# Fetching the weights of the second layer earlier, and v of the first batch one z transpose sooner, in a fused attention and mixer kernel

## Chip, cores, metric

One core of one Trainium2 chip. The metric is the device time of one execution in microseconds (us). Medians and ranges are over several executions. "PE" is the matmul engine, "DVE" VectorE, "ACT" ScalarE, "POOL" GpSimd, "SP" SyncE. Two kinds of DMA matter: copies issued by POOL (queue q0) and transposes issued by SP (queue q1). A DMA "lands" when its last data has arrived. "Half clock" is a stretch in which the clock records of the trace grant PE half its speed. L260 in a profile is line 260 of the kernel.

## The reference

```python
def attn(u, v, z):                    # u, v: (8, 3136, 256), z: (8, 3136, 64)
    scores = z @ z.T / S              # per batch
    return u * (np.maximum(scores, 0) ** 2 @ v)

def moe(x, U, V, w_ch1, w_ch2):       # U: (3136, 32), V: (32, 3136), w: (256, 1024), (1024, 256)
    u = x + (x.T @ U @ V).T
    return u + np.maximum(u @ w_ch1, 0) @ w_ch2
# out = moe(attn(u, v, z), ...)
```

The second layer of a batch needs U, V, w1 and w2. Here it runs beside the attention of the next batch, so the weights are first needed when batch 1 begins, about 125 us into the program.

## The kernel before

A batch is 25 tiles of 128 rows ("steps" i = 0 to 24). The scores are symmetric, so only half the blocks are computed (`A`); the other half (`strip`) is made by DMA transposes, one per step, four steps ahead of use. z of the next batch is transposed by two DMA transposes (`z_half`, `z_turn`). In the second layer, `ut` is made of `x_bf` by further DMA transposes. All transposes are issued by SP in program order; all copies from memory by POOL in program order.

```python
def turn(b, o):                                   # SP: 1536 packets of 256 bytes
    strip = strip_pool.tile([P, HALF, P], BF16)   # 5 buffers
    transpose(out=strip, in_=A[o][:, P:])

def start_up():                                   # the first 8 outputs of batch 0, all at once
    load_z(0, parts); load_v(0, v_parts[0])
    double_z(0, parts)
    turn_z(0, parts)                              # three z transposes
    mark = small.tile(...)
    nc.gpsimd.tensor_copy(out=mark[:1, :1], in_=zT[:1, NF - 1, :1])   # POOL waits for the last of them
    for part in v_parts[1:]:
        load_v(0, part)
    # ... u of the first outputs, z of batch 1, scores and the first four outputs ...
    # ... the next four outputs ...

weights = weight_steps()    # w1, U, V piece, V piece, put, put, w2, V tail, put, put, put, copies
start_up()
weights = dict(zip((8, 9, 13, 14, 15, 16, 17, 18, 19, 20, 21, 22), weights))   # one per step of batch 0
# ...
        z_load, z_double, z_half, z_turn = (1, 5, 7, 11) if b else (None, 9, 11, 13)
        v_at = (1, 3, 4, 5, 7, 8, 10, 11, 12) if b else (8, 9, 10, 14, 15, 16, 17, 18, 19)   # v of the next batch
# scores from the new z begin in step 15 of batch 0:
next_first = ahead_of((15, 15, 15, 16, 16, 17, 18, 19, 20, 21, 22, 23), (15, 16, 17, 18, 19, 20, 21))
```

## Time and profile before

Median 1078.82 us over the first three runs (1078.75 to 1081.77). From batch 2 on a batch takes 126.8 us and PE hardly waits; what there is to gain lies before 145 us.

| wait of PE, kernel before | at (us) | length (us) |
|---|---|---|
| first z transpose | 10.12 | 10.12 |
| v of batch 0 | 17.68 | 1.88 |
| two strip transposes | 69.33, 74.60 | 1.66 + 2.29 |
| second z transpose of batch 1 | 89.36 | 10.21 |
| first ut transpose (second layer of batch 0) | 139.03 | 3.90 |

The timeline of PE of the kernel before, cut to the matmuls that waited for a DMA: start, length, what, and in brackets the idle time before it and what ended that.

```profile
10.12 1.03 PE L260 MATMUL ps<-zT 64*128 64x512 bf16 x4 [10.12 <-DMA zT<-z_bf]
...
17.68 0.50 PE L333 MATMUL ps<-v,v 64*128 64x256 bf16 x6 [1.88 <-DMA v<-in_v_dram]
...
69.33 0.28 PE L333 MATMUL ps<-v,strip 64*128 64x256 bf16 x2 [1.66 <-DMA strip<-A]
...
74.60 1.48 PE L333 MATMUL ps<-v,strip 64*128 64x256 bf16 x24 [2.29 <-DMA strip<-A]
...
89.36 0.24 PE L260 MATMUL ps<-zT 64*128 64x64 bf16 x2 [10.21 <-DMA zT<-z_bf]
...
139.03 0.59 PE L455 MATMUL ps<-ut,w_bf 128*128 128x512 bf16 x1 [3.90 <-DMA ut<-x_bf]
```

The chain of waits of the kernel before between 55 and 92 us, its end: it leaves PE at 61.57 and runs through a strip transpose, 4.2 us of PE and the z transpose.

```profile
61.57 12.98 DMA strip<-A
74.56 0.04 issue
74.60 4.23 PE ps L333 x74
78.83 0.64 SPq L295
79.47 0.05 issue
79.52 9.79 DMA zT<-z_bf
```

The timeline of SP of the kernel before, same stretch: the second number is how long the issues kept SP, with the waits between them where a line has several (in the first line SP waits 5.2 us, until 56.16, for a semaphore). An issue takes 1.4 us when the DMA is free (1.42 us at 26.17, with a DMA share of 0.03 from 26 to 27 us); here the z transpose alone keeps SP for 7.80 us.

```profile
49.36 22.38 SPq L295 DMA_TRANSPOSE strip<-A  x4
71.79 3.39 SPq L184 DMA_TRANSPOSE zT<-z_bf  x1
75.28 4.18 SPq L295 DMA_TRANSPOSE strip<-A  x2
79.52 7.80 SPq L184 DMA_TRANSPOSE zT<-z_bf  x1
```

What the DMA engines did from 80 to 84 us (queue: packets, MB, share of 16 engines' time): copies had 94%, and all transposes together, the one that PE waits for among them, moved 0.02 MB. Times of packets overlap in the trace, so that shares can add up to more than 100%.

```profile
q0 software_dynamic: 292, 0.52, 94.1%
q1 hardware_dynamic: 121, 0.02, 20.4%
```

Three stretches of 40 us of the kernel before. After the length come the busy times (and counts) of PE, weight loads, DVE, ACT and POOL, then the granted PE clock, the DMA share and GB/s. DMA is used least in the first of them, and PE least in the second.

```profile
10.00:50.00 40.00, 33.16 (x458) 25.99 (x460) 27.53 (x54) 33.38 (x53) 7.44 (x15) 1.00 0.77 147
50.00:90.00 40.00, 24.64 (x416) 19.93 (x414) 18.75 (x38) 18.28 (x28) 8.85 (x16) 0.91 1.18 174
90.00:130.00 40.00, 39.62 (x686) 33.05 (x682) 29.97 (x53) 27.08 (x38) 10.42 (x17) 0.96 1.22 189
```

### The profile page before, as it was taken

The page shows a single profiled execution, that of the slowest core. Times are in us where ns is not written, and L with a number is a line of the kernel's source. Part 1 is how long each engine was busy: PE and PEld are TensorE (multiplying, and loading weights), DVE is VectorE, ACT ScalarE, POOL GpSimd, SP SyncE. Part 2 cuts the span into 40 slices and gives each one's busy share as a digit, 9 for nine tenths or more (in the row PEclk, how much of TensorE's full clock was granted, in tenths as well). Part 3 has the DMA queues.
Part 4 walks back from the last instruction along what each step waited for, and adds up shares of the span by engine and source line. Part 5 has one row for each costly group of instructions (what it writes and reads, how often), then busy time and mean ns, then how long its engine had stood idle before and what let it go on. Part 6 is the DMA issues. An engine that isn't in the chain of part 4 may idle for free.

```text
span 1078.5 us, 31056 instructions
## 1 busy us (share of the span) xinstructions
PE 1010.8 (94%) x13789; PEld 792.3 (73%) x13829; DVE 525.7 (49%) x937; ACT 611.7 (57%) x814; POOL 179.0 (17%) x332
## 2 busy tenths in 40 slices
PE   5876989999999999999999999999999999999896
PEld 3665857788677877778777886778777887778564
DVE  4755734456443554446454465435554465432331
ACT  5955655466664666556654666556655566542253
POOL 3022201211121111211212111211112110111011
PEclk9998989999999999999999999999999999999898
DMA  8799999969989798979989789997989887588231
GB/s 142 145 170 190 172 163 169 172 140 169 162 173 176 150 183 163 164 159 167 177 167 173 147 167 160 175 179 150 179 158 171 168 160 134 129 150 168 57 98 64
DMA packets 417174, 168.71 MB, mean 156 GB/s; under 512 B 392768, under 2 KB 402640, under 8 KB 417040
## 3 DMA queue, kind: packets, MB, share of 16 engines
q1 hardware_dynamic: 386464, 96.77, 56.7%
q0 software_dynamic: 30576, 69.96, 27.7%
q8 instruction: 108, 1.77, 0.7%
q14 instruction: 26, 0.21, 0.1%
HBM read 61.88 MB, written 25.69 MB: 81 GB/s over the span
## 4 chain that ended last, share of the span: by engine, by line
PE 77%; DVE 7%; DMA 6%; ACT 5%; issue 3%; POOL 1%; SPq 0%; POOLq 0%; ACTq 0%; DVEq 0%
PE ps L333 40%; PE ps L486 15%; PE ps L455 15%; PE ps L260 5%; ACT A L273 3%; DVE x_bf L435 2%; DMA strip<-A 2%; DVE both L348 2%; DVE A L275 2%; DMA ut<-x_bf 1%; DMA zT<-z_bf 1%; PE ps L401 1%; DVE x_bf L351 1%; ACT both L347 1%; PE ps L421 1%
## 5 line engine op out<-in xcount | busy, mean ns | idle before, releaser
L273 ACT ACTIVATE A<-ps 128x832 bf16<-128x832 f32 (+8 forms) x469 | 351.6, 763 | 184.8 <-PE ps L260 175.5
L333 PE MATMUL ps<-v,A 64*128 64x256 bf16 x5064 | 357.9, 270 | 5.7 <-DVE x_bf L435 2.3
L275 DVE TENSOR_TENSOR A<-A 128x832 bf16<-128x832 bf16 (+8 forms) x469 | 240.5, 524 | 219.1 <-ACT A L273 216.2
L333 PE MATMUL ps<-v,strip 64*128 64x256 bf16 x4612 | 319.3, 269 | 3.9 <-DMA strip<-A 3.9
L462 ACT ACTIVATE relu<-ps 128x1024 bf16<-128x1024 f32 (+2 forms) x224 | 203.5, 917 | 190.5 <-PE ps L455 190.5
L333 PEld LDWEIGHTS <-A 64*128 64x128 bf16 x5064 | 251.5, 94 | 64.0 <-issue 27.3
L333 PEld LDWEIGHTS <-strip 64*128 64x128 bf16 x4612 | 233.3, 94 | 37.8 <-DMA strip<-A 4.5
L455 PE MATMUL ps<-ut,w_bf 128*128 128x512 bf16 (+2 forms) x856 | 205.1, 357 | 11.6 <-DMA ut<-x_bf 6.7
L486 PE MATMUL ps<-w_bf,relu 128*128 128x256 bf16 x1600 | 205.9, 273 | 1.0
L486 PEld LDWEIGHTS <-relu 128*128 128x128 bf16 x1600 | 153.8, 98 | 49.5 <-issue 9.3
L260 PE MATMUL ps<-zT 64*128 64x416 bf16 (+9 forms) x933 | 155.7, 317 | 23.3 <-DMA zT<-z_bf 20.3
L497 DVE TENSOR_TENSOR o_sb<-ps,x_bf 128x512 f32<-128x512 f32 (+1 forms) x104 | 69.7, 670 | 221.2 <-PE ps L486 221.2
L455 PEld LDWEIGHTS <-w_bf 128*128 128x128 bf16 x896 | 87.2, 99 | 69.6 <-issue 18.0
L317 POOL DMA_DIRECT2D u_sb<-in_u_dram x96 | 53.5, 558 | 494.3 <-DVE x_bf L351 440.7
L504 POOL DMA_DIRECT2D out_dram<-o_sb x96 | 52.4, 546 | 330.9 <-DVE o_sb L497 330.9
L347 ACT COPY both<-ps 128x512 f32<-128x512 f32 (+1 forms) x104 | 58.8, 566 | 64.7 <-PE ps L333 64.6
L348 DVE TENSOR_TENSOR both<-ps,both 128x512 f32<-128x512 f32 (+1 forms) x104 | 69.3, 666 | 53.0 <-ACT both L347 52.5
L260 PEld LDWEIGHTS <-zT 64*128 64x128 bf16 x933 | 53.1, 95 | 32.1 <-DMA zT<-z_bf 20.6
L351 DVE TENSOR_TENSOR x_bf<-both,u_sb 128x512 bf16<-128x512 f32 (+1 forms) x104 | 69.8, 671 | 6.3 <-DMA u_sb<-in_u_dram 2.7
L435 DVE TENSOR_TENSOR x_bf<-ps,x_bf 128x512 bf16<-128x512 f32 (+1 forms) x112 | 65.4, 625 | 15.4 <-PE ps L421 15.3
L195 POOL DMA_DIRECT2D v<-in_v_dram x61 | 34.1, 566 | 0.0
L421 PE MATMUL ps<-t_sb,V_bf 64*128 64x256 bf16 x200 | 22.6, 273 | 9.9 <-DVE both L348 8.3
(33 smaller groups left out, 134.2 us busy)
## 6 DMA issues: line engine op xcount, KB each, us to landing
u_sb<-in_u_dram POOLq DMA_DIRECT2D x96, 256.0 KB, 3.5
out_dram<-o_sb POOLq DMA_DIRECT2D x96, 256.0 KB, 3.0
v<-in_v_dram POOLq DMA_DIRECT2D x57, 192.0 KB, 5.9
strip<-A SPq DMA_TRANSPOSE x196, 4.9
z_c<-in_z_dram POOLq DMA_DIRECT2D x7, 384.0 KB, 5.5
w_bf<-in_moe_w_ch_dram POOLq DMA_DIRECT2D x2, 512.0 KB, 7.8
u_sb<-in_u_dram POOLq DMA_DIRECT2D x16, 64.0 KB, 2.2
ut<-x_bf SPq DMA_TRANSPOSE x56, 3.5
```

The source lines that it names most:

```text
L260: mm(out=ps[:, k, :n], lhsT=zT[halves[k], j, :], rhs=zT_flat[halves[k], c : c + n], start=True, stop=True,)
L273: nc.scalar.activation(out=dst, in_=src, func=AF.Relu, scale=sc)
L275: nc.vector.tensor_tensor(out=dst, in0=dst, in1=dst, op=ALU.mult)
L333: mm(out=acc[t0][h][:, (o - t0) * D : (o - t0 + 1) * D], lhsT=w[halves[h]], rhs=v_both[b % 2][halves[h], j, :], start=start, stop=stop, **kw,)
L347: nc.scalar.copy(out=both[:, :w], in_=banks[1][:, :w])
L348: nc.vector.tensor_tensor(out=both[:, :w], in0=banks[0][:, :w], in1=both[:, :w], op=ALU.add)
L351: nc.vector.tensor_tensor(out=x_at(b, t0, n), in0=split(both[:, :w]), in1=u_sb[:, :n, :].rearrange("p t (a c) -> p t a c", c=P), op=ALU.mult,)
L435: nc.vector.tensor_tensor(out=q, in0=split(ps[h][:, : len(ks) * D]), in1=q, op=ALU.add)
L455: mm(out=ps[:, i, :w], lhsT=w1_bf[:, db, (hp + i) * P : (hp + i + 1) * P], rhs=uT[c][:, db, len(chunks[c]) * P - w :], start=(db == 0), st ...
L462: nc.scalar.activation(out=relus[c][:, hp : hp + 2, :w], in_=ps[:, :, :w], func=AF.Relu)
L486: mm(out=ps[:, k * D : (k + 1) * D], lhsT=relus[c][:, ht, q : q + P], rhs=w2_bf[:, ht, :], start=(ht == 0), stop=(ht == NH - 1),)
L497: nc.vector.tensor_tensor(out=o_sb[:p, :nk, :].rearrange("p t (a c) -> p t a c", c=P), in0=split(ps[:p, : nk * D]), in1=x_at(b, t, nk)[:p] ...
```

## The change

Copies that nobody needs before 115 us are moved out of the crowded stretch into the one where DMA had gaps: w1, U and the two large pieces of V go behind z of batch 1 (about 20 us), w2 behind the first four outputs (about 33 us). The marker that holds v of batch 0 back waits for the second z transpose in place of the third. One piece of v of batch 1 moves from step 14 to 12, and the later ones one step sooner.

```diff
+            lambda: wide(w2_bf, moe_w_ch2),          # order of weight_steps: w2 fifth
             lambda: put(0, 0, FIRST),
             lambda: put(0, FIRST, NF),
-            lambda: wide(w2_bf, moe_w_ch2),
...
-        nc.gpsimd.tensor_copy(out=mark[:1, :1], in_=zT[:1, NF - 1, :1])
+        nc.gpsimd.tensor_copy(out=mark[:1, :1], in_=zT[:1, 7, :1])
...
             load_z(1, WHOLE)
+        for s in weights[:4]:
+            s()
...
             load_u(0, o)                             # u of outputs 5 to 8
+        weights[4]()
...
-    weights = dict(zip((8, 9, 13, 14, 15, 16, 17, 18, 19, 20, 21, 22), weights))
+    weights = dict(zip((14, 15, 16, 17, 18, 19, 20), weights[5:]))
...
-        v_at = (...) if b else (8, 9, 10, 14, 15, 16, 17, 18, 19)
+        v_at = (...) if b else (8, 9, 10, 12, 14, 15, 16, 17, 18)
```

More of the change, by code (lines that the diff above doesn't have):

```diff
@@ L683 @@
         soon = next_at if b else next_first
-        v_at = (1, 3, 4, 5, 7, 8, 10, 11, 12) if b else (8, 9, 10, 14, 15, 16, 17, 18, 19)
+        v_at = (1, 3, 4, 5, 7, 8, 10, 11, 12) if b else (8, 9, 10, 12, 14, 15, 16, 17, 18)
         v_at = dict(zip(v_at, V_PARTS))
```

## The prediction

> **What bounds the kernel now.** The page shows PE busy 1010.8 of 1078.5 us. From batch 2 on, PE hardly waits: the same matmul recurs at 264.42, 391.26, 518.31 us (126.8 us a batch). In the PE timeline, waits ended by DMA: 10.12 us (first z transpose), 1.88 us at 17.68 (v of batch 0), 1.66 us at 69.33 and 2.29 us at 74.60 (strip transposes), 10.21 us at 89.36 (second half of the z transpose of batch 1), 3.90 us at 139.03 (first ut transpose). Two are followed by half clock (clock records: 82.9-93.2 and 137.5-144.4 us), costing about 1.9 and 2.7 us more. Batch 1 (131.54 to 264.42) takes 132.9 us against 126.8 later: 6.0 us.
>
> **Why.** Transposes from SP share the DMA engines with copies from POOL. Uncontended, a strip transpose lands in 3.7 us; between 56 and 88 us it takes 8.8 to 13.1, while w1 (7.3 us to landing), U (10.2), two V pieces (6.7, 7.9) and v pieces of batch 1 (8 to 10) are under way. SP issues in order, and an issue that takes 1.4 us free takes 5.3, 6.6 and 7.8 us there; the z transpose that PE needs at 78.7 is issued at 79.52 and lands at 89.31. [...] copies of 1.5 to 6 KB packets leave the 256-byte transpose packets almost nothing at 80-84 us. w2 (8.4 us at 101 us) does the same to strips (9 to 13 us), a backlog reaching to the ut transpose at 131.5.
>
> **What the change moves.** No arithmetic. w1, U and V go to about 20-35 us, w2 to about 34-44 us. There strips are needed only from 42.4 us on. v of batch 0 is released by the second z transpose (10.97) instead of the third (12.35). One v piece of batch 1 moves from the 9th to step 12, later ones one step earlier; V's copies on DVE come a little sooner (1.1 us each).
>
> **Sum on the critical path.** v sooner: -1.4. The two strip waits: -3.9. z wait of 10.2: the earliest issue is about 69.5 us in the new time, behind two strips, and I let about 2 us of wait stay: -8.3. Its half clock: -1.9, less 0.3 left. ACT/strip wait at 117.8: -0.4. Batch 1 to the steady pace: -6.0, less 0.5. New contention at 25-45 us: allow +1. Total about -20.8.
>
> Predicted **1058.0 us**, range 1054.5 to 1064.0. Faster by over 2%: 0.47; within 2%: 0.52; slower: 0.01.
>
> **Seen in the profile if right.** PE's wait for v at 17.7 falls to about 0.5 us. w1, U, V land by 36 us, w2 by 46. Strips at 55-75 us land in 4 to 7 us; SP's issue of the second z transpose comes near 69-70; PE's wait for it is 0 to 4 us. No half clock near 83-93 and 137-144. PE's ut wait gone; batch 1 takes about 127 us.
>
> **What would make it wrong.** Strips of the first outputs (needed from 42 us) or the u pairs held up by w1/w2: a new wait at 42-53 us. The three v pieces and five strips at 54-70 us alone keep the DMA full: z wait stays at 5 us or more and the clock drops. [...]

## The result

Changed kernel: median **1066.20 us** (1065.36 to 1066.61, 4 runs) against 1079.48 us (1078.75 to 1081.77, 4 runs), ratio 0.9872 (95% interval 0.9855 to 0.9890). A ratio here is the mean time of one kernel's fast runs over that of the other's of the same rounds, so it is not quite the ratio of the medians. Executions over 1.5% slower than the fastest of the same kernel are left out of the means. The gain is 13.3 us by the medians; predicted were 20.8. 1066.2 lies outside the predicted range of 1054.5 to 1064.0.

The waits for v, for strips and for ut are gone; of the z wait 6.24 us are left. PE's timeline of the changed kernel, the two matmuls that waited for a DMA before 145 us:

```profile
9.55 1.04 PE L260 MATMUL ps<-zT 64*128 64x512 bf16 x4 [9.55 <-DMA zT<-z_bf]
...
79.44 0.23 PE L260 MATMUL ps<-zT 64*128 64x64 bf16 x2 [6.24 <-DMA zT<-z_bf]
```

The chain of waits of the changed kernel, where it leaves PE; a single transpose is left in it.

```profile
67.09 3.08 PE ps L333 x54
70.17 1.18 SPq L295
71.35 0.05 issue
71.41 0.03 issue
71.44 7.95 DMA zT<-z_bf
```

SP of the changed kernel: the six transposes ahead of the second z transpose are issued in 17 us (54.51 to 71.44) in place of 23 (56.16 to 79.52), but the z transpose itself keeps SP for 5.87 us.

```profile
54.51 9.82 SPq L295 DMA_TRANSPOSE strip<-A  x3
64.38 1.91 SPq L184 DMA_TRANSPOSE zT<-z_bf  x1
66.39 4.96 SPq L295 DMA_TRANSPOSE strip<-A  x2
71.44 5.87 SPq L184 DMA_TRANSPOSE zT<-z_bf  x1
```

POOL of the changed kernel. Look at 69.05 and 69.57: a u load and two v pieces go out 1.3 to 2.4 us ahead of the z transpose at 71.44.

```profile
62.57 0.60 POOL L195 DMA_DIRECT2D v<-in_v_dram  x1
67.17 0.55 POOL L317 DMA_DIRECT2D u_sb<-in_u_dram  x1 [4.00 <-DVE A L275]
69.05 0.54 POOL L317 DMA_DIRECT2D u_sb<-in_u_dram  x1 [1.32 <-DVE x_bf L351]
69.57 1.09 POOL L195 DMA_DIRECT2D v<-in_v_dram  x2
81.59 0.85 POOL L317 DMA_DIRECT2D u_sb<-in_u_dram  x1 [10.93 <-DVE x_bf L351]
```

The same three stretches of the changed kernel: the first now uses the DMA as fully as the next (1.15 for 0.77) and PE did no less in it; PE's busy time in the second rose from 24.6 to 32.6 us.

```profile
10.00:50.00 40.00, 35.15 (x480) 27.59 (x478) 29.15 (x58) 35.02 (x55) 12.04 (x23) 1.00 1.15 192
50.00:90.00 40.00, 32.58 (x533) 26.45 (x529) 24.54 (x46) 23.32 (x37) 7.91 (x14) 0.91 1.17 190
90.00:130.00 40.00, 39.00 (x648) 30.79 (x646) 28.19 (x50) 27.79 (x38) 8.11 (x14) 1.00 1.01 175
```

Where the time of the two profiled runs (1078.5 and 1063.6 us) differs, by four points that both traces have:

| from | to | before | changed | difference |
|---|---|---|---|---|
| start | first matmul on a strip | 42.40 | 40.75 | -1.65 |
| there | end of the z wait | 46.96 | 38.69 | -8.27 |
| there | first matmul of the second layer (x U) | 36.75 | 36.56 | -0.19 |
| there | the same in batch 2 | 132.88 | 127.25 | -5.63 |
| there | end | 819.5 | 820.4 | +0.8 |

The last line is one wait of 1.66 us for a ut transpose at 761 us, partly made up at the end; waits like it stand near 760 us in the profiles of two of the runs below (e14 2.16 us, e18 1.71 us) and not in the others, so it is taken as chance.

### The profile page after: what moved, and what is told of

Read it like the earlier page. It is cut to its first block, busy times and chain, and to the rows that moved or that the text cites. A ratio compares the mean times of both kernels' runs of the same rounds, so it can differ in the third digit from the quotient of the medians.

```text
span 1063.6 us, 31097 instructions
## 1 busy us (share of the span) xinstructions
PE 1010.7 (95%) x13829; PEld 791.3 (74%) x13829; DVE 525.3 (49%) x937; ACT 611.4 (57%) x814; POOL 178.7 (17%) x332
## 4 chain that ended last, share of the span: by engine, by line
PE 81%; DVE 7%; ACT 5%; issue 3%; DMA 2%; POOL 1%; SPq 0%; POOLq 0%; ACTq 0%; DVEq 0%
PE ps L333 43%; PE ps L486 16%; PE ps L455 15%; PE ps L260 6%; ACT A L273 3%; DVE x_bf L435 3%; DVE both L348 2%; DVE A L275 2%; DMA zT<-z_bf 1%; PE ps L401 1%; DVE x_bf L351 1%; ACT both L347 1%; PE ps L421 1%; ACT relu L462 1%; DMA ut<-x_bf 1%
## 5 line engine op out<-in xcount | busy, mean ns | idle before, releaser
L333 PE MATMUL ps<-v,A 64*128 64x256 bf16 x5064 | 358.6, 271 | 5.7 <-DVE x_bf L435 2.3
L333 PE MATMUL ps<-v,strip 64*128 64x256 bf16 x4612 | 319.9, 270 | 0.0
L333 PEld LDWEIGHTS <-A 64*128 64x128 bf16 x5064 | 251.7, 94 | 64.5 <-issue 27.1
L333 PEld LDWEIGHTS <-strip 64*128 64x128 bf16 x4612 | 233.2, 94 | 34.1 <-issue 0.2
```

Source lines behind the costliest of these rows:

```text
L333: mm(out=acc[t0][h][:, (o - t0) * D : (o - t0 + 1) * D], lhsT=w[halves[h]], rhs=v_both[b % 2][halves[h], j, :], start=start, stop=stop, **kw,)
```

## The experiments

All times are medians of fast runs; "z wait" is PE's wait for the second z transpose of batch 1 in the one profile taken of that run. The medians of the kernel before, taken beside them, were 1077.5 to 1080.1.

| run | edit | us | ratio to before (95%) | z wait |
|---|---|---|---|---|
| changed kernel | | 1066.20 | 0.9872 (0.9855-0.9890) | 6.24 |
| e15_after_again | the same again | 1065.01 | 0.9879 (0.9846-0.9911) | 5.91 |
| e17_before_again | kernel before again | 1077.49 | 1.0000 (0.9974-1.0026) | 8.82 |
| e1_mark_only | before + marker | 1076.06 | 0.9965 (0.9931-0.9998) | 8.17 |
| e2_w1uv_only | before + w1, U, V early | 1072.03 | 0.9934 (0.9904-0.9963) | 7.29 |
| e3_w2_only | before + w2 early | 1071.17 | 0.9921 (0.9899-0.9943) | 8.05 |
| e14_before_no_w | before, no weights fetched (wrong result) | 1067.20 | 0.9900 (0.9867-0.9933) | 5.63 |
| e4_v_at_old | changed, v pieces at old steps | 1065.11 | 0.9870 (0.9846-0.9894) | 6.30 |
| e5_v1415_late | changed, last five v pieces two steps later | 1062.19 | 0.9833 (0.9804-0.9861) | 3.96 |
| e16_e5_again | the same again | 1063.33 | 0.9865 (0.9833-0.9897) | 5.22 |
| e13_skip2 | changed, first two of those five not fetched (wrong result) | 1062.27 | 0.9856 (0.9823-0.9888) | 5.04 |
| e6_v_all_late | changed, all v pieces later | 1076.60 | 0.9967 (0.9917-1.0017) | none |
| e9_v_dense | changed, six v pieces sooner, two more of them before the z transpose | 1074.56 | 0.9972 (0.9937-1.0008) | 12.91 |
| e7_zturn12 | changed, z transpose a step sooner | 1065.85 | 0.9865 (0.9832-0.9898) | 7.35 |
| e12_late_zturn12 | e5 + e7 | 1072.01 | 0.9939 (0.9904-0.9975) | 1.60 |
| e8_use16 | changed, new z used a step later | 1063.46 | 0.9840 (0.9808-0.9872) | 3.39 |
| e18_use16_again | the same again | 1064.50 | 0.9881 (0.9860-0.9901) | 2.96 |
| e10_late_use16 | e5 + e8 | 1068.04 | 0.9888 (0.9836-0.9940) | slow run |
| e11_late12_use16 | e10, one more v piece later | 1068.60 | 0.9934 (0.9868-1.0001) | 1.45 |

### The parts of the change, one at a time

e1_mark_only: the kernel before with the new marker.

```diff
-        nc.gpsimd.tensor_copy(out=mark[:1, :1], in_=zT[:1, NF - 1, :1])
+        nc.gpsimd.tensor_copy(out=mark[:1, :1], in_=zT[:1, 7, :1])
```

> The kernel before with only the marker moved: v of batch 0 is begun behind the second z transpose. Theory (parts add up, v is on the chain): PE's wait for v at 17.7 us falls from 1.9 to under 0.6 us and everything up to 60 us comes 1.4 us sooner; the waits for strips (1.7 and 2.3), for z (10.2) and for ut (3.9) stay; total -1.4 us, 1078 us. Rival (the early gain is swallowed by the later DMA-bound stretch, which ends when the DMA work is done, not when PE is ready): the z wait grows by about 1.4 us and the total is unchanged.

The ratio is 0.9965, some 3 us less. The wait for v is gone from the profile, as expected; strip waits of 0.64 and 2.12 us, a z wait of 8.17 and a ut wait of 4.03 us are left. That the total fell speaks against the rival, though the interval barely leaves out 1. The "1.4 us sooner up to 60 us" cannot be read from this profile, as a half clock at 33.1 to 39.9 us made the first strip matmul come at 43.24. That the gain is over 1.4 us is not explained by this part; see the spread of the kernel before, below.

e2_w1uv_only: the kernel before with w1, U and V early, w2 in its place.

```diff
             load_z(1, WHOLE)
+        for s in weights[:4]:
+            s()
...
-    weights = dict(zip((8, 9, 13, 14, 15, 16, 17, 18, 19, 20, 21, 22), weights))
+    weights = dict(zip((15, 16, 17, 18, 19, 20, 21, 22), weights[4:]))
```

> The kernel before with only w1, U and the two V pieces fetched early; w2 and the v pieces of batch 1 where they were. Theory (copies between 56 and 88 us starve the transposes): both strip waits (1.7, 2.3) are gone, the z wait falls from 10.2 to between 4 and 7 us, the ut wait of batch 1 (w2 at about 90 us still causes a backlog) stays above 2 us; total -7 to -10 us. Rival (w1, U, V were not the cause, SP's own transposes fill the DMA): strip waits stay and the z wait stays above 8 us.

Both strip waits are gone, the z wait is 7.29 us (just above what was expected), the ut wait of 3.06 us stays; ratio 0.9934, about 7 us. The rival is out for the strips: w1, U and V did hold them up.

e3_w2_only: the kernel before with w2 behind the first four outputs.

```diff
             load_u(0, o)
+        weights.pop(6)()
...
-    weights = dict(zip((8, 9, 13, 14, 15, 16, 17, 18, 19, 20, 21, 22), weights))
+    weights = dict(zip((8, 9, 13, 14, 15, 16, 18, 19, 20, 21, 22), weights))
```

> The kernel before with only w2 fetched early. Theory (w2's backlog reaches batch 1): the strip waits and the z wait (10.2) stay as before, since w2 came after them; strips at 100 to 125 us land in under 7 us in place of 9 to 13; the ut wait of 3.9 us in batch 1 and the half clock after it go, batch 1 takes 127 us; total -5 to -6 us. Rival (the ut wait comes from z and v of batch 2, fetched at 126 us): the ut wait stays near 3.9 us and the total moves by under 1 us.

The ut wait is gone and batch 1 takes 127.2 us: w2 was its cause and the rival is out. The total fell by about 8.5 us, more than expected, and the z wait was 8.05, though w2 came after it in the kernel before. The ratios of the three parts alone add to -1.8%, while all together give -1.3%.

e17_before_again was to show whether the 10.2 us of the one profile of before was a fixed quantity.

> The kernel before once more, unaltered, for a second profile of it: the single changes that should not touch the z wait of batch 1 (v of batch 0 sooner; w2 early, which is fetched after that wait) showed z waits of 8.2 and 8.0 us against 10.2 in the only profile of before. If the 10.2 was one draw of a quantity that varies, this profile shows a z wait between 8 and 11 us and strip waits that differ by over 0.5 us from 1.7 and 2.3; if those changes really acted on it, it shows 10 to 10.5 us again. Time 1074 to 1083 us, ratio to itself within 0.4% of 1.

```profile
72.68 0.39 PE L333 MATMUL ps<-v,strip 64*128 64x256 bf16 x2 [3.25 <-DMA strip<-A]
...
90.31 0.23 PE L260 MATMUL ps<-zT 64*128 64x64 bf16 x2 [8.82 <-DMA zT<-z_bf]
```

In this second profile of the same program (PE's timeline) the z wait is 8.82 us, with one strip wait of 3.25. So the 10.2 was one draw, and the z waits of e1 and e3 say nothing about their edits. The wait for v is a draw too: 1.88, 0.93, 0.64, 1.20 and 1.70 us in the five profiles with the old marker (before, e17, e2, e3, e14), and none over 0.6 us in those with the new one. The kernel before runs between 1073.3 and 1083.9 us over all its runs here, the changed one between 1063.9 and 1066.7.

e14_before_no_w gives a wrong result: the kernel before with constants for the weights, so that none of these copies is made anywhere.

```diff
-            pool_dma(out=w_bf, in_=w.rearrange("(t p) d -> p t d", p=P))
+            pass                      # w1, w2: memset at the start; U likewise
...
-            pool_dma(out=flat[:, :n], in_=moe_V[:, p0 * NF : p0 * NF + n])
+            nc.gpsimd.memset(flat[:, :n], 0.01)
```

> WRONG RESULT ON PURPOSE: the kernel before with w1, w2, U and V not fetched at all (constants in their place), everything else as before: what the best possible move of these copies can give. Theory (moving them to the start was as good as deleting them, and the rest of the gain is the start): it comes out 1.5 to 2.5 us slower than the changed kernel, since its v of batch 0 still begins late: 1067 to 1069 us, z wait 6 to 7 us, ut wait of batch 1 gone, wait for v at 17.7 us still 1.9. Rival (the copies at 20 to 45 us spill into the later stretch): it is faster than the changed kernel, with a z wait below 5 us.

1067.20 us, 2.2 us slower than the changed kernel on the same chip (1065.01), with a z wait of 5.63, no ut wait in batch 1 and the old wait for v (1.70). So moving these copies gave as much as deleting them. That the 2.2 us left over are the sooner v fits, but is not shown: the intervals overlap, and the profile of e14 has the chance wait of 2.16 us at 762 us. For the weights the change works to its limit; what is left of the z wait has other causes.

### What holds the remaining z wait

e4_v_at_old, e5_v1415_late, e6_v_all_late and e9_v_dense change one line of the changed kernel, the steps at which v of batch 1 is fetched:

```diff
-        v_at = (...) if b else (8, 9, 10, 12, 14, 15, 16, 17, 18)
+        v_at = (...) if b else (8, 9, 10, 14, 15, 16, 17, 18, 19)    # e4
+        v_at = (...) if b else (8, 9, 10, 12, 16, 17, 18, 19, 20)    # e5
+        v_at = (...) if b else (16, 17, 18, 19, 20, 21, 22, 23, 24)  # e6
+        v_at = (...) if b else (8, 9, 10, 11, 12, 13, 14, 15, 16)    # e9
```

> The changed kernel with the v pieces of batch 1 at their old steps (8, 9, 10, 14, 15, ...), so that one piece of 192 KB less lies before the second z transpose. Theory (each copy ahead of it costs its own time on the DMA engines, about 1.6 us a piece): z wait 6.2 falls to about 4.6 us, total -1.6 us or a little more against the changed kernel if the half clock goes too. Rival 1 (the transposes alone fill the DMA, copies do not matter): z wait stays at 6.2. Rival 2 (what remains is the place of the z transpose in SP's order): z wait stays at 6.2.

A miss: without the piece of step 12 the z wait is 6.30, not 4.6. The strips before it did land sooner (5.4 to 7.8 us against 6.4 to 8.7), and the z transpose was issued at 70.63 in place of 71.44, but the two pieces of steps 14 and 15 went out beside it at 70.11 and 70.64, and it took 9.4 us to land in place of 8.0. A copy does not simply add its own time. (The 1.6 us a piece, here and for e5, and the 1.2 to 1.6 for e9, are estimates. In the trace of the kernel before a piece of 192 KB is 128 packets of 1.5 KB; packets of this size took 0.194 us in the mean from 56 to 88 us, which makes 1.55 us on 16 engines, and 0.166 us over the whole program, which makes 1.33.)

> The changed kernel with the v pieces of steps 14 and 15 (issued at 69.6 and 70.1 us, just ahead of the second z transpose at 71.4) and all later ones moved two steps on, behind that transpose. Theory (copies ahead of the z transpose cost it their own DMA time, 1.6 us a piece): z wait 6.2 falls to about 3 us, the half clock after it shrinks or goes, total -3 to -5.5 us against the changed kernel. Rival 1 (the transposes alone fill the DMA): z wait stays above 5 us. Rival 2 (place in SP's order): z wait stays above 5 us.

The z transpose lands in 5.7 us, z wait 3.96 us; when the same kernel was profiled again (e16) it was 5.22. So the two pieces beside the z transpose cost 0.7 to 2.3 us of the wait, by which of the profiles are compared, less than expected, and most of it stays. In landing alone they cost more: 5.7 and 4.8 us (e5, e16) against 8.0 and 7.8 (changed kernel, e15). But e16 issued the transpose only at 74.32, after 71.44 and 72.03, and why is not settled.

> The changed kernel with all nine v pieces of batch 1 at steps 16 to 24, none before the second z transpose. Theory (copies): strips at 54 to 70 us land in under 5 us, SP issues the second z transpose at about 69 us, z wait falls to 0 to 2 us; batch 1 may then wait for v. Rival 1 (the transposes alone fill the DMA): strips still land in 6 to 8 us and the z wait stays above 4 us. Rival 2 (place in SP's order: behind the strips of steps 11 and 12, both waiting for PE): a wait of 2 to 3 us stays, since the issue cannot come before step 12 ends at 68 us and two transposes ahead of it take 4 us.

Without any v piece before it the z transpose is issued at 67.86, lands at 73.87, and PE needs it at 73.88: the wait is gone. SP's timeline, to be read against the two above:

```profile
48.51 12.86 SPq L295 DMA_TRANSPOSE strip<-A  x4
61.42 2.13 SPq L184 DMA_TRANSPOSE zT<-z_bf  x1
63.65 3.83 SPq L295 DMA_TRANSPOSE strip<-A  x2
67.86 3.06 SPq L184 DMA_TRANSPOSE zT<-z_bf  x1
```

SP is 3.6 us ahead of where it stood in the changed kernel (71.44). This rules out both rivals: neither the transposes alone nor their order in SP keeps PE waiting. (The u loads, two of which go out at 67 to 70 us as well, were moved in no run.) The four pieces of steps 8 to 12 delay the strips, these delay SP, and so the z transpose; the two of steps 14 and 15 then slow it down. But the nine copies must be made, and they now meet the strips after step 16. PE's timeline of the same run, later:

```profile
93.63 0.35 PE L260 MATMUL ps<-zT 64*128 64x416 bf16 x2 [1.40 <-ACT A L273]
...
102.55 0.53 PE L260 MATMUL ps<-zT 64*128 64x416 bf16 x2 [5.50 <-ACT A L273]
...
113.02 0.34 PE L260 MATMUL ps<-zT 64*128 64x384 bf16 x2 [2.64 <-ACT A L273]
```

ACT may not overwrite a block of A before the strip transpose that reads it is done (four waits of ACT for strips, 14.9 us in all before 170 us), and PE waits for ACT. The kernel is 10 us slower than the changed one, by its median; the profiled run was the quickest of four (1070.84 to 1082.44).

> The changed kernel with the v pieces of batch 1 packed closer (steps 8 to 16), so that two more pieces of 192 KB lie between step 11 and the second z transpose: the dose the other way from moving two away, which took the z wait from 6.2 to 4.0. Theory (each copy in flight beside the z transpose costs it its DMA time, 1.2 to 1.6 us): z wait 8 to 10 us. Rival (only what SP has in its own order counts): z wait stays at 6.2.

The other way: two more pieces ahead of the z transpose give a z wait of 12.91 us, more than expected (8 to 10). The first z transpose alone took 15.5 us to land. The wait follows the copies, but not in proportion.

e13_skip2 gives a wrong result: the changed kernel without the two pieces of steps 14 and 15 (batch 1 multiplies left-over data), against e5, which only puts them off.

```diff
     def load_v(b, part):
         t0, t1 = part
+        if b == 1 and t0 in (12, 15):
+            return
```

> WRONG RESULT ON PURPOSE: the changed kernel without the two v pieces of steps 14 and 15 of batch 1 at all (batch 1 multiplies with left-over data). Against the run in which the same two pieces are only put off by two steps, all else in place. Theory (the z wait is set by the copies that stand beside the z transpose): z wait about 4 us, as with the pieces put off. Theory that DMA work put off must be paid later: this one is faster than the run that puts them off, by up to their own 2 to 3 us, about 1060 us. Rival (putting off is free, DMA has room later): both take the same time, within 1 us.

1062.27 us, z wait 5.04, more than the 4 expected; e16 on the same chip 1063.33 and 5.22. Putting these two off costs about 1 us by the medians against leaving them out, which is not clear of noise. Without any copy beside it the z transpose landed in 4.5 us, but it was issued at 73.53, 1.5 to 2.1 us later than in the two profiles of the changed kernel. So most of the z wait stays without these two pieces, as a late issue.

### Place and time of the z transpose

e7_zturn12 issues the second z transpose a step sooner; e8_use16 needs it a step later.

```diff
-        z_load, z_double, z_half, z_turn = (1, 5, 7, 11) if b else (None, 9, 11, 13)
+        z_load, z_double, z_half, z_turn = (1, 5, 7, 11) if b else (None, 9, 11, 12)     # e7
-    next_first = ahead_of((15, 15, 15, 16, 16, 17, ...
+    next_first = ahead_of((16, 16, 16, 16, 16, 17, ...                                   # e8
```

> The changed kernel with the second z transpose placed one step sooner in SP's order (12 in place of 13), and the scores of batch 0 that must precede it squeezed into one step less. Rival 2 (place in SP's order): z wait 6.2 falls by the time of a step, about 2.7 us, to 3 to 4 us; the half clock may go; total -3 to -5 us. Theory (copies): falls only by the one strip transpose that is no longer ahead, about 2 us. If PE or ScalarE has no room for the squeezed scores, steps 8 to 11 grow by 1 to 2 us.

The z transpose is issued at 70.47 and takes 11.2 us to land, beside a u load and two v pieces; z wait 7.35 us, time unchanged (1065.85). With those copies beside it a sooner place in SP's order gave nothing; in e12 below, with them away, it shortens the wait.

> The changed kernel with the first use of the new z put off from step 15 to step 16 (three pieces of scores more in step 16). DMA work and its order are unchanged. Theory (the z transpose lands at 79.4 us whatever PE does): PE gets one step more, about 2.7 us, before it waits, so the z wait falls from 6.2 to about 3.5 us; the total falls by 2.7 us plus what the clock gives (up to 2). Rival (the time is bound by the DMA up to about 90 us): PE waits as long a little later, for strips in step 15 or 16, and the total stays within 1 us.

The z wait falls to 3.39 us as expected, because PE needs z later; the landing (82.23) is no sooner. Ratio 0.9840.

> The changed kernel with the first use of the new z in step 16, once more with five rounds. If PE's need, not the landing, is what this moves, the z wait is 3 to 4 us again and the time 1060 to 1064 us, 2 to 4 us under the changed kernel's 1065 to 1066 and with a spread under 5 us; if it is paid later in some runs, the times spread over more than 5 us.

Again z wait 2.96 us and no half clock after it, but a strip wait of 0.81 came up; 1064.50, ratio 0.9881, no better than the changed kernel in its own runs. The two results for this edit differ by as much as the edit was to gain, so whether it gains anything stays open.

### Attempts at a version that beats both

> The changed kernel with the v pieces of steps 14 and 15 behind the z transpose and the first use of the new z in step 16. Theory (the two gains add, since one moves the landing and the other moves PE's need of it): z wait 6.2 - 2.3 - 2.8 = about 1.1 us, no half clock after it, total 1057 to 1060 us. Rival (the stretch is DMA-bound to about 90 us, so PE waits for the next strips instead): new strip waits in steps 16 to 19, total stays at 1062.

The fast runs were 1060.52, 1068.04 and 1068.82; a fourth, slow, took 1079.46, and the profile fell in it. One of the fast runs is among the best (only e8 had a faster one, 1059.82), but the three miss the expected 1057 to 1060: no reliable gain. The 1079.46 may belong to the same spread, as e11's 1077.97 counts as fast.

> As the run with late v and first use in step 16, with the piece of step 12 late too (steps 8, 9, 10, then 16 to 21). Theory: z transpose lands another 0 to 1.5 us sooner (moving this piece alone to a later step did not lower the z wait, because two other pieces then stood beside the z transpose; now none does), z wait 0 to 1 us, total 1056 to 1060 us. Rival (v pieces pushed too late collide with strips, as with all nine pieces late, where ScalarE waited 5 us): new waits of ScalarE or PE in steps 18 to 24, total not below the run with step 12 kept.

z wait 1.45 us, but a strip wait of 0.84 and a ut wait of 5.13 us appear, and the runs spread from 1064.39 to 1077.97. No gain.

> The changed kernel with the v pieces of steps 14 and 15 late and the second z transpose one step sooner in SP's order. In the run with the sooner transpose alone it was issued at 70.5 us and took 11 us to land (z wait 7.4). Theory (it was starved by u and the two v pieces issued at the same time, so the place in SP's order gave nothing): without them it lands within 6 us, z wait 1 to 3 us. Rival (the sooner place gives nothing in itself, because the strip before it ties it down): z wait as with the late v pieces alone, about 4 us.

z wait 1.60 us as expected, against 3.96 and 5.22 with the late pieces alone, and then, in PE's timeline of the same run:

```profile
76.40 0.20 PE L260 MATMUL ps<-zT 64*128 64x64 bf16 x2 [1.60 <-DMA zT<-z_bf]
...
87.77 0.35 PE L260 MATMUL ps<-zT 64*128 64x416 bf16 x2 [2.42 <-ACT A L273]
...
99.77 0.36 PE L260 MATMUL ps<-zT 64*128 64x416 bf16 x2 [4.13 <-ACT A L273]
```

With them go 1.06 us at 92.28 and 2.03 at 109.49. Strips issued from 80 to 94 us took 11 to 15 us to land, and ACT waited 13.5 us for them from 75 to 115 us, as in e6. The total is about 6 us worse than the changed kernel. What PE gains at the z transpose it gives back here.

> The changed kernel once more, unaltered, beside the others on one chip: 1065 to 1067 us; z wait 6 to 6.5 us, followed by half clock. If the z wait or the half clock differs by over 2 us from the first profile, the residue is not a fixed quantity of this program but varies from run to run.

1065.01 us, z wait 5.91, half clock from 76.4 to 83.3 us: the residue of the changed kernel is steady.

> The changed kernel with the v pieces of steps 14 and 15 and all later ones two steps on, once more, with five rounds beside the changed kernel: if the first result holds, 1061 to 1063 us, 3 to 4.5 us faster than the changed kernel, z wait about 4 us. If instead what is put off is paid later in some runs (as in the runs with the first use in step 16), the times spread over more than 4 us and the median is within 2 us of the changed kernel's.

1063.33 us (1062.77 to 1064.62), 1.7 us under the changed kernel on the same chip, less than the first time. Of the two edits of the changed kernel that were measured twice, it is the only one whose measurements both came out below the changed kernel's, by 0.1 to 0.4% in the ratio to before, with intervals that overlap: a small gain at best.

## Why the prediction was wrong

Right, with the numbers of the profile after:

- Mechanism and place. Copies starve transposes between 56 and 138 us (strips issued from 56 to 79 us took 8.8 to 13.1 us to land and those from 100 to 108 us, around w2, 9.2 to 13.0, against 3.7 us for the one at 26.17), and moving w1, U, V and w2 to the start ends the strip waits (predicted -3.9, measured -3.95), the ut wait and the slow batch 1 (predicted -5.5, measured -5.63). e2 and e3 show which copy did which, and e14 that the move was as good as deleting the copies.
- The start: predicted -1.4; measured -1.65 up to the first strip, of which the first z transpose, 0.57 us sooner in this run, is not the change's, so that about -1.1 is left. w1, U and V landed by 30.04 us and w2 by 42.69, with no new wait, so the +1 allowed for new contention was not needed.

Wrong: the step "**behind two strips, and I let about 2 us of wait stay: -8.3. Its half clock: -1.9, less 0.3 left**". The wait left was 6.24 us (5.91 in the second profile), so the term was -4.0. With it the half clock came back: 77.5 to 84.4 us in the clock records, of which PE worked 4.9 us (79.44 to 84.35). About 2.5 us of them were lost, where before it was 1.9 of 3.8 us; these are estimates, half of the time worked at the granted 0.5 (ten matmuls of L333 took 1.23 to 1.27 us there, 0.71 us at 84.64, after it). Together -9.9 was predicted and about -3.4 came, 6.5 us less. The gain was overstated by 7.5 us by the medians and by 5.9 between the two profiled runs (14.9 us), so this term makes up nearly all of it. (The terms of the prediction as written add up to -20.1, not -20.8.) The prediction had named this outcome under "What would make it wrong", as v pieces and strips that keep the DMA full, a z wait of 5 us or more and a dropping clock; the sum was made without it.

What the runs showed in place of that term:

1. The four v pieces of steps 8 to 12 were taken to leave strips at 4 to 7 us; they took 6.4 to 8.7, SP fell behind, and the z transpose went out at 71.44 in place of 69.5. e6, without any v piece, issues at 67.86 and has no wait. This looks like the larger part, as 4 to 5 us stay when only the other two pieces are gone (e5, e13, e16). Against the prediction's own figures the split is more even: the wait was 4.2 us above the 2 allowed, the later issue is 1.9 of that, and the rest must lie in the landing or in when PE needs z, for which the prediction gives no figure.
2. The pieces of steps 14 and 15 were expected behind the z transpose (the prediction counts three v pieces from 54 to 70 us; the trace has four, at 54.11, 54.63, 62.57 and 69.57), as the u load ahead of them in POOL's order was thought (the text does not spell it out) to wait for the output that ends at 73 us. It waits for the one before, whose last work on DVE began at 68.33, so they left at 69.57 and 70.10, just ahead of the z transpose. e5, e13 and e16 put this at 1 to 2 us of the wait, and the traces 2.1 to 3.4 us of the landing.
3. The DMA time of copies does not simply add up, as the expectations of e4, e5 and e9 (not the prediction itself) took it to: a piece less before the z transpose gave nothing, two more gave 6.7 us.

The prediction also took the 10.2 us z wait of one profile as given; a second profile of the same program had 8.8.

What stays open: why the three parts alone give more than all together (the spread of the kernel before, 10 us, is larger than the excess), how the z wait divides between the pieces ahead of the z transpose and those beside it, and how much of it the stretches with nearly no transpose packets, described below, cost.

## What to carry to other kernels

Move a copy to where the DMA has gaps and nobody waits; measured against a run without that copy, the move can be worth all of it (1065.01 us against 1067.20 without the copies, e14). When DMA is nearly full for a whole stretch (a share of 1.17 from 50 to 90 us here), putting other copies off inside that stretch mostly moves the wait (e6 and e12, 10 and 6 us slower than the changed kernel). And before sizing a wait for a DMA, find what every issue around it really waits for, and profile the same program twice, since a DMA wait was a draw here and not a constant (10.21 and 8.82 us for the same one).

## What else the traces show

- Copies of 1.5 to 6 KB packets left the 256-byte packets of transposes next to nothing: 94.1% of the engines and 0.52 MB against 20.4% and 0.02 MB, at 80 to 84 us in the kernel before. How the engines choose between the queues is not shown. A mix can also move less than one kind alone: transposes alone moved 287 GB/s (70.0 to 71.2 us in the changed kernel, DMA share 1.28), the mix at 110 to 120 us in the kernel before 143, with the DMA share at 1.26.
- Stretches with nearly no transpose packets follow packets of the queue that the trace calls "instruction". In the changed kernel a 16 KB packet of this queue, of 1.1 us, at 75.6 us is followed by 1.4 us (76.1 to 77.5) in which nearly no transpose packet starts and some take up to 1.49 us, where 0.018 us is usual; it fell on the very z transpose that PE waited for. Of 65 places in that profile where transpose packets took over 0.7 us (packets under 0.5 us apart taken as one place), 54 begin within 3 us after one of its 108 instruction packets; of all moments 30% do. In e13, with no copy beside this z transpose, 1.1 us of its 4.5 pass in the same way after such a packet at 74.46. As one starts during this transpose (at 84.11 us in the kernel before), or less than 0.4 us before it, in every profile here, it does not explain the differences between runs. Seen, not tested by an experiment. The DMA queues of the changed kernel from 75.3 to 77.5 us, GB/s in 40 slices and then the queues:

```profile
GB/s 279 293 293 298 289 582 275 270 265 275 265 275 234 238 47 23 14 5 0 0 0 0 0 0 0 0 9 9 5 9 14 5 9 9 9 14 9 9 9 14
...
q1 hardware_dynamic: 901, 0.22, 152.4%
q8 instruction: 1, 0.02, 3.2%
```

- Half clock lasted 10.24, 6.83 and 6.83 us in the kernel before, 6.83 and 3.41 us in the changed one and once 13.65 us in e9 (clock records, before the end of the program). It also came without a wait of PE of 3.41 us: at 1018.2 us in the kernel before, within a wait of 2.68 us, and from 32 to 35 us in the profiles of e15, e16 and e18, where no wait near it is over 1.1 us. In the 3.41 us before these switches PE was busy for 0.30 (before) and 0.42 to 0.50 (e15, e16, e18) of the time. How much idle time it takes is not shown.
